# Who picks the place of a tile: the pool that hands out tiles, or the kernel's own plan

## Chip, core and metric

The kernel runs on one core of one Trainium2 chip. The metric is the device time of one execution in microseconds (us); the time before is the median of three runs.

## What is computed

All arrays are float32. Attention with a sigmoid instead of a softmax runs over 4 batches of 12 heads, 448 tokens and 64 columns a head. Its output, seen as 1792 tokens by 768, goes through two feed-forward layers.

```python
scores = scale * np.matmul(q, k.transpose(0, 1, 3, 2)) - np.log(S)
attn = 1.0 / (1.0 + np.exp(-scores))
x = np.matmul(attn, v)                                # then (B*S, 768)
...
xn = x / np.sqrt(np.mean(x * x, -1, keepdims=True) + 1e-06) * rms_g
g = xn @ w_gate                                       # 768 x 1536
y = ((g / (1.0 + np.exp(-g))) * (xn @ w_val)) @ w_out # 1536 x 768
...
h = y @ w_in                                          # 768 x 2048
out = (h - np.tanh(h)) @ w_out2                       # 2048 x 768
```

## The kernel before

**The work.** Attention (some 150 us) takes the heads in pairs; the rest of the time goes to five kinds of job: `Ag` and `Av` (gate and value), `B` (the first layer's output), `C` and `D` (the second layer). Each kind runs for batches 0 and 1 and then for batches 2 and 3. A matrix product of 2 by 2 blocks is mostly made with seven block products instead of eight, from sums and differences of the blocks (`S1` to `S4` of the weights, `T1` to `T4` of the tokens). Each float32 operand is split into a high and a low part, and a product takes three matmuls of 128 x 128 by 448 columns (lines 1081, 1136, 1161). TensorE (PE) does these; ScalarE (ACT) and VectorE (DVE) split operands, form sums, empty the PSUM banks and apply the functions.

**The transfers.** SyncE (SP) issues loads and most stores in the order of its queue: raw weights (line 488), prepared weights that were put into DRAM and come back (stores at lines 589 and 632, loads at 636, 644 and 672), spilled tokens (line 875). GpSimd (POOL) issues the loads and stores of the weights of the second products (`wB`, `wD`, line 589) and the sums that a DMA adds up in DRAM (`sumB`, `sumD`, `out`, line 959).

**The places.** A tile stands in one place of four pools: `unit` has 72 places of 128 x 448, `part` 20 of 128 x 768, `raw` 2, and `ps` the 8 PSUM banks. In the program's names, part_3881 is one `part` tile. When a new tile takes the place of an old one, its first writer waits until the last instruction that used the old tile is done; for an old tile that a DMA stores, until that DMA has landed.

**The order.** `Plan` keeps each piece of work with what it reads and writes. `lay` replays the work with a modelled duration for each piece and a table of ranks (`ORDER`), and gives each piece an engine and a start; the pieces are then issued in the order of these starts. For the places it counts: per pool a sorted list of the times, in its model, at which places come free. It takes the earliest, but which place of the chip a tile stands in it doesn't say. Line 409 asks a pool of 72 places under one tag for a tile, and the layer that hands out tiles picks one:

```python
return Slot(kind, lambda: pool.tile(shape, dt, tag=tag, name=tag))
```

Of the kernel before, what the change touches and what calls it, by code (L numbers as in the profile page):

```python
# [9 lines left out]
F32 = mybir.dt.float32  # L10
# [7 lines left out]
PSUM = bass.MemoryType.PSUM  # L18
# [4 lines left out]
P = 128  # L23
# [22 lines left out]
N_UNIT, N_MOE, N_RAW, N_PART = 72, 40, 2, 20  # L46
# [15 lines left out]
def numbers(text):  # L62
    d = [DIGITS[c] for c in text if c in DIGITS]
    return [4096 * d[i] + 64 * d[i + 1] + d[i + 2] for i in range(0, len(d), 3)]


class Slot:


    def __init__(self, kind, make):  # L70
        self.kind, self.make, self.tile = kind, make, None
        self.uses = []

    def __getitem__(self, part):
# [3 lines left out]
class Plan:  # L78
# [21 lines left out]
    def issue(self):  # L100
        work = self.work
        self.graph()
        for n, e in self.lay([ORDER_UNIT * n for n in numbers(ORDER)]):
            for s in self.slots[n]:
                s.tile = s.tile or s.make()
            work[n][1](e)

    def graph(self):
# [19 lines left out]
    def lay(self, rank):  # L128

        work, needs, users, slots, n_work = self.work, self.needs, self.users, self.slots, len(self.work)  # L130
        missing = [len(ds) for ds in needs]
        end, where, start_of = [None] * n_work, [None] * n_work, [None] * n_work
        taken, since = set(), {}
        kind_order = {}
        for n in range(n_work):
            for s in slots[n]:
                if s.kind and s.uses[0] == n:
                    kind_order.setdefault(s.kind, []).append(s)
        kind_at = {k: 0 for k in kind_order}
        free = {pool: [0.0] * size for pool, (size, _) in self.room.items()}  # L140
        held = {k: 0 for k in kind_order}
        pool_of = {k: pool for pool, (_, kinds) in self.room.items() for k in kinds}
        cap = {k: c for _, kinds in self.room.values() for k, c in kinds.items()}
        streams = {}
        for n, w in enumerate(work):
            if w[4]:
                streams.setdefault(w[4], []).append(n)
        stream_at = {s: 0 for s in streams}
        left = {}
        clock = {e: 0.0 for e in self.ENGINES}  # L150
        port = moving = 0.0
        waiting = sorted(n for n in range(n_work) if not missing[n])
        oldest, done = 0, [False] * n_work
        issued = 0

        def places(n):

            t, want = 0.0, {}
            for s in slots[n]:
                if not s.kind:  # L160
                    continue
                if s in taken:
                    t = max(t, since[s])
                    continue
                k = s.kind
                i = kind_at[k] + want.get(k, 0)
                if kind_order[k][i] is not s:
                    return None
                want[k] = want.get(k, 0) + 1
            for k, x in want.items():  # L170
                if held[k] + x > cap[k]:
                    return None
                f = free[pool_of[k]]
                if len(f) < x:
                    return None
                t = max(t, f[x - 1])
            return t

        while issued < n_work:
            cands = []  # L180
            while done[oldest]:
                oldest += 1
            for n in waiting:
                if n > oldest + self.WINDOW:
                    break
                engines, _, _, _, stream, _ = work[n]
                if stream and streams[stream][stream_at[stream]] != n:
                    continue
                if n > oldest + self.CLOSE and any(s.kind in self.CLOSELY and s not in taken for s in slots[n]):
                    continue  # L190
                t_place = places(n)
                if t_place is None:
                    continue
                ways = []
                for e, (ns, uses_port) in engines.items():
                    r = t_place
                    for d in needs[n]:
                        r = max(r, end[d] + (self.OTHER if where[d] != e else self.SAME if e != "PE" else 0))
                    if uses_port:
                        r = max(r, port)  # L200
                    start = max(clock[e], r)
                    ways.append((start + ns, start, n, e, uses_port))
                cands.append(min(ways, key=lambda w: w[0]))
            if not cands:
                raise RuntimeError(f"no work can start; the oldest is {oldest}")
            soonest = min(c[1] for c in cands) + SOON
            finish, start, n, e, uses_port = min((c for c in cands if c[1] <= soonest), key=lambda c: rank[c[2]])
            clock[e] = finish
            if uses_port:
                port = finish  # L210
            if work[n][5]:
                moving = max(finish + self.BEGIN, moving) + work[n][5]
                end[n] = moving + self.LAND
            else:
                end[n] = finish
            start_of[n], where[n], done[n] = start, e, True
            waiting.remove(n)
            for s in slots[n]:
                if s in taken:
                    continue  # L220
                taken.add(s)
                if s.kind:
                    kind_at[s.kind] += 1
                    held[s.kind] += 1
                    since[s] = free[pool_of[s.kind]].pop(0)
            for s in slots[n]:
                left[s] = left.get(s, len(s.uses)) - 1
                if s.kind and not left[s]:
                    held[s.kind] -= 1
                    bisect.insort(free[pool_of[s.kind]], max(end[u] for u in s.uses) + self.OTHER)  # L230
            if work[n][4]:
                stream_at[work[n][4]] += 1
            for u in users[n]:
                missing[u] -= 1
                if not missing[u]:
                    bisect.insort(waiting, u)
            issued += 1
        return [(n, where[n]) for n in sorted(range(n_work), key=lambda n: (start_of[n], n))]
# [127 lines left out]
def tile_sigmoid_attention_moe_moe(  # L366
# [16 lines left out]
    ENG = {"PE": nc.tensor, "ACT": nc.scalar, "DVE": nc.vector, "POOL": nc.gpsimd, "SP": nc.sync}  # L383

    const = ctx.enter_context(tc.tile_pool(name="const", bufs=1))
    unit_p = ctx.enter_context(tc.tile_pool(name="unit", bufs=N_UNIT))
    raw_p = ctx.enter_context(tc.tile_pool(name="raw", bufs=N_RAW))
    part_p = ctx.enter_context(tc.tile_pool(name="part", bufs=N_PART))
    norm_p = ctx.enter_context(tc.tile_pool(name="norm", bufs=4))
    ps_p = ctx.enter_context(tc.tile_pool(name="ps", bufs=8, space=PSUM))  # L390
    dram_p = ctx.enter_context(tc.tile_pool(name="spill", bufs=1, space=DRAM))

    plan = Plan({
# [12 lines left out]
        return {e: ({"SP": 400, "ACT": 540, "POOL": 870 if added else 540}[e], False)}  # L406

    def slot(kind, pool, shape, dt, tag):
        return Slot(kind, lambda: pool.tile(shape, dt, tag=tag, name=tag))

    def bank(kind="mm"):
        return slot(kind, ps_p, [P, 512], F32, "ps")

    def unit(kind, dt=F32):
        return slot(kind, unit_p, [P, S], dt, "unit")

    def part_of(kind, shape, dt=F32):
        return slot(kind, part_p, shape, dt, "part")
# [26 lines left out]
    def whole_bank(ps):  # L445

        nc.tensor.matmul(ps[:, :S], lhsT=mark[:, :P], rhs=mark, start=True, stop=True)
# [12 lines left out]
    for names, ph in (  # L460
# [3 lines left out]
        for bs in BATCHES:  # L464
            n = n_sets(ph)
# [768 lines left out]
    nc.gpsimd.memset(ones, 1.0)  # L1234

    for n in range(N_WARM):
        warm = ps_p.tile([P, 512], F32, tag="ps", name="ps")
        whole_bank(warm)
    nc.scalar.activation(expo[:, 0:1], ones[:, 0:1], AF.Sigmoid)
    nc.gpsimd.memset(expo, -0.5)  # L1240
# [74 lines left out]
    for j in range(len(jobs)):  # L1315
        ahead = conv(j + AHEAD) + rows_late.get(j - ROWS_AT, []) + [lambda: load(j + 2 * AHEAD)]
        plan.copies_by = "ACT"
        kind = kind_of(j)
# [5 lines left out]
        n = 2 if kind == PLAIN else HELD  # L1324
# [73 lines left out]
```

## Time and profile before

| | us |
|---|---|
| median of three runs (lowest to highest) | 1031.68 (1030.65 to 1034.58) |
| the profiled execution, its own time | 1031.29 |
| its span, from the first to the last instruction | 1029.5 |
| PE busy with matmuls | 1015.3 |
| DVE busy | 789.7 |
| ACT busy | 675.0 |
| POOL busy | 153.6 |

1.8 us of the profiled execution's time lie outside its span. The mean granted clock of PE was 0.996 of full speed. Engines work at the same time, so the busy times don't add up; idle time of an engine counts where the busiest one, PE, waits for it.

### The profile page before, as it was taken

The page shows a single profiled execution, that of the slowest core. Times are in us where ns is not written, and L with a number is a line of the kernel's source. Part 1 is how long each engine was busy: PE and PEld are TensorE (multiplying, and loading weights), DVE is VectorE, ACT ScalarE, POOL GpSimd, SP SyncE. Part 2 cuts the span into 40 slices and gives each one's busy share as a digit, 9 for nine tenths or more (in the row PEclk, how much of TensorE's full clock was granted, in tenths as well). Part 3 has the DMA queues.
Part 4 walks back from the last instruction along what each step waited for, and adds up shares of the span by engine and source line. Part 5 has one row for each costly group of instructions (what it writes and reads, how often), then busy time and mean ns, then how long its engine had stood idle before and what let it go on. Part 6 is the DMA issues. An engine that isn't in the chain of part 4 may idle for free.

```text
span 1029.5 us, 15331 instructions
## 1 busy us (share of the span) xinstructions
PE 1015.3 (99%) x5261; PEld 878.5 (85%) x5261; DVE 789.7 (77%) x1284; ACT 675.0 (66%) x1232; POOL 153.6 (15%) x217
## 2 busy tenths in 40 slices
PE   9999999999998999999999999999999999999998
PEld 4555479999997999899999999999998999999997
DVE  5578998877865878886875857999787986675766
ACT  6777956676674566684774747877675766675742
POOL 4231010000040051111012030000303300003030
PEclk9999999999998999999999999999999999999999
DMA  9587578778689599879859479585949782749493
GB/s 325 199 319 266 195 250 290 255 235 315 217 223 331 199 219 344 301 253 404 313 187 245 138 138 306 179 317 166 256 129 285 214 245 61 253 114 209 124 225 135
DMA packets 102573, 241.41 MB, mean 234 GB/s; under 512 B 11520, under 2 KB 59712, under 8 KB 102496
## 3 DMA queue, kind: packets, MB, share of 16 engines
q1 hardware_dynamic: 77840, 172.53, 49.0%
q0 software_dynamic: 24512, 67.84, 26.2%
q8 instruction: 41, 0.67, 0.3%
q14 instruction: 36, 0.29, 0.1%
q10 hardware_dynamic: 144, 0.07, 0.0%
HBM read 150.74 MB, written 89.66 MB: 234 GB/s over the span
## 4 chain that ended last, share of the span: by engine, by line
PE 86%; issue 6%; DMA 4%; DVE 2%; POOL 1%; ACT 1%; SPq 0%; POOLq 0%; DVEq 0%
PE ps L1136 43%; PE ps L1081 28%; PE ps L814 6%; PE ps L757 5%; PE ps L1161 3%; DMA wD<-part 2%; DMA sumB<-unit 1%; PE ps L778 1%; PE ps L798 1%; POOL sumB L959 1%; DMA part<-in_qkt 1%; PE ps L850 0%; DVE unit L1017 0%; DVE part L522 0%; DVE unit L888 0%
## 5 line engine op out<-in xcount | busy, mean ns | idle before, releaser
L1136 PE MATMUL ps<-unit,part 128*128 128x448 f32 x2520 | 521.5, 365 | 7.6 <-ACT unit L439 5.0
L1136 PEld LDWEIGHTS ps<-unit,part 128*128 128x128 f32 x2520 | 473.2, 188 | 50.2 <-ACT unit L439 7.9
L1081 PE MATMUL ps<-unit,part 128*128 128x448 f32 x1512 | 311.4, 364 | 0.0
L1081 PEld LDWEIGHTS ps<-unit,part 128*128 128x128 f32 x1512 | 283.4, 187 | 22.3
L522 DVE TENSOR_TENSOR part<-part 128x768 fp32r<-128x768 f32 (+1 forms) x244 | 215.7, 890 | 64.9 <-ACT part L439 53.6
L439 ACT COPY unit<-ps 128x448 f32<-128x448 f32 x291 | 151.2, 540 | 127.7 <-PE ps L1136 57.3
L439 ACT CAST part<-part 128x768 fp32r<-128x768 f32 (+1 forms) x236 | 183.3, 788 | 30.9 <-DVE part L607 7.7
L888 DVE TENSOR_TENSOR unit<-unit 128x448 fp32r<-128x448 f32 x252 | 152.5, 619 | 34.5 <-ACT unit L439 18.1
L439 ACT CAST unit<-unit 128x448 fp32r<-128x448 f32 x257 | 143.3, 576 | 30.6 <-DVE unit L1000 11.9
L1017 DVE TENSOR_TENSOR unit<-ps,unit 128x448 f32<-128x448 f32 x168 | 104.0, 622 | 41.4 <-PE ps L1081 17.5
L766 ACT ACTIVATE unit<-ps 128x448 f32<-128x448 f32 x168 | 81.3, 582 | 25.9 <-PE ps L757 14.3
L893 DVE TENSOR_TENSOR unit<-unit 128x448 f32<-128x448 f32 x144 | 86.2, 619 | 5.8 <-DMA unit<-sumB 2.8
L511 DVE SCALAR_TENSOR_TENSOR part<-raw,zero 128x768 uint32<-128x768 uint32 x68 | 64.8, 953 | 31.4 <-ACT zero L439 18.7
L439 ACT CAST zero<-raw 128x768 f16<-128x768 bf16 x56 | 60.5, 1080 | 11.9 <-DMA raw<-in_w_out 4.2
L959 POOL DMA_DIRECT2D sumB<-unit x48 | 41.9, 958 | 156.7 <-ACT unit L439 101.8
L814 PE MATMUL ps<-unit,part 128*64 128x448 f32 x288 | 59.5, 547 | 0.5 <-ACT unit L766 0.5
L1161 PE MATMUL ps<-unit,part 128*128 128x448 f32 x288 | 59.2, 364 | 0.0
L1161 PEld LDWEIGHTS ps<-unit,part 128*128 128x128 f32 x288 | 54.0, 187 | 4.2
L959 POOL DMA_DIRECT2D out<-unit x36 | 30.9, 927 | 174.9 <-DVE unit L1017 165.7
L757 PEld LDWEIGHTS ps<-unit 64*128 64x128 f32 x396 | 35.7, 184 | 19.1 <-ACT unit L766 9.7
L757 PE MATMUL ps<-unit 64*128 64x448 f32 x396 | 47.9, 376 | 0.0
L439 ACT COPY ps<-ps 128x448 f32<-128x448 f32 x36 | 18.7, 520 | 43.4 <-PE ps L1136 43.3
(54 smaller groups left out, 491.8 us busy)
## 6 DMA issues: line engine op xcount, KB each, us to landing
raw<-in_w_out POOLq DMA_DIRECT2D x28, 768.0 KB, 7.4
part<-wD SPq DMA_DIRECT2D x56, 384.0 KB
part<-wB SPq DMA_DIRECT2D x36, 384.0 KB
part<-wC SPq DMA_DIRECT2D x33, 384.0 KB
raw<-in_w_in SPq DMA_DIRECT2D x16, 768.0 KB
wC<-part SPq DMA_DIRECT2D x30, 384.0 KB
sumB<-unit POOLq DMA_DIRECT2D x48, 224.0 KB, 8.8
wD<-part POOLq DMA_DIRECT2D x28, 384.0 KB, 6.4
```

The lines of the kernel that those rows point to most:

```text
L439: add(engines, lambda e: (nc.scalar.copy if e == "ACT" else nc.vector.tensor_copy)(to(), of()), reads, writes)
L522: add({**dve(n, psum=False), **pool(n)}, lambda e: ENG[e].tensor_sub(lo(), of(), hi().bitcast(F32)), [*reads, *kh], [*kl])
L757: nc.tensor.matmul(ps[i].tile[:, :S], lhsT=k_of(w, b, c, i), rhs=x.tile[rows, :S], start=q == 0, stop=q == len(terms) - 1)
L766: add(act(S, psum=True), lambda e: nc.scalar.activation(to.tile, ps.tile[:, :S], AF.Sigmoid, bias=-math.log(S), scale=1.0 / math.sqrt(D)), ...
L814: nc.tensor.matmul(ps.tile[HEADS[i], :S], lhsT=v_of(v, b, c, i), rhs=a[c][i].tile, start=opens and c == 0, stop=not opens and c == MAIN - ...
L888: add({**pool(S), **dve(S, psum=False)}, lambda e: ENG[e].tensor_sub(t["l"].tile, of.tile, t["h"].tile.bitcast(F32)), [of["t"], kh], [kl])
L893: add({**dve(S, psum=False), **pool(S)}, lambda e: ENG[e].tensor_sub(t.tile, x.tile, y.tile), [x["t"], y["t"]], [t["t"]])
L959: add(queue("POOL", True), lambda e: nc.gpsimd.dma_start(out=d.tile, in_=t.tile, accum_op=ALU.add), [t["t"], d["t"]], [d["t"]], moved=move ...
L1017: add(dve(S), lambda e: nc.vector.tensor_add(t.tile, ps.tile[:, :S], t.tile), [ps["t"], t["t"]], [t["t"]])
L1081: nc.tensor.matmul(ps.tile[:, :S], lhsT=part(a), rhs=x[b].tile, start=n in (1, 5) and kp == 0 and q == 0, stop=kp == n_kp - 1 and q == 2, ...
L1136: nc.tensor.matmul(ps.tile[:, :S], lhsT=part(a), rhs=x[b].tile, start=n in ((1, 2, 5) if opening else (1, 5)) and i == 0 and q == 0, stop= ...
L1161: nc.tensor.matmul(ps.tile[:, :S], lhsT=wt, rhs=a[p].tile, start=start and i == 0, stop=stop and i == 2, skip_group_check=True)
```

## The change

Every place gets a tag of its own with one buffer (`unit0` to `unit71`, and so on), and the plan's list of free places holds, beside the modelled time at which a place comes free, which place it is. A tile gets the place at the head of that list. The numbers of places in each pool, the table `ORDER` and the rules of the plan stay. New lines number two, so a line 439 of before is line 441 after.

```diff
-        self.kind, self.make, self.tile = kind, make, None
+        self.kind, self.make, self.tile, self.place = kind, make, None, None
...
-                s.tile = s.tile or s.make()
+                s.tile = s.tile or (s.make(s.place) if s.kind else s.make())
...
-        free = {pool: [0.0] * size for pool, (size, _) in self.room.items()}
+        free = {pool: [(0.0, -1, i) for i in range(size)] for pool, (size, _) in self.room.items()}
+        n_freed = 0
...
-                t = max(t, f[x - 1])
+                t = max(t, f[x - 1][0])
...
-                    since[s] = free[pool_of[s.kind]].pop(0)
+                    since[s], _, s.place = free[pool_of[s.kind]].pop(0)
...
-                    bisect.insort(free[pool_of[s.kind]], max(end[u] for u in s.uses) + self.OTHER)
+                    bisect.insort(free[pool_of[s.kind]], (max(end[u] for u in s.uses) + self.OTHER, n_freed, s.place))
+                    n_freed += 1
...
-    unit_p = ctx.enter_context(tc.tile_pool(name="unit", bufs=N_UNIT))
+    unit_p = ctx.enter_context(tc.tile_pool(name="unit", bufs=1))
...
-        return Slot(kind, lambda: pool.tile(shape, dt, tag=tag, name=tag))
+        return Slot(kind, lambda place: pool.tile(shape, dt, tag=f"{tag}{place}", name=tag))
...
-        warm = ps_p.tile([P, 512], F32, tag="ps", name="ps")
+        warm = ps_p.tile([P, 512], F32, tag=f"ps{n % 8}", name="ps")
```

In the built program every engine has the same instructions on the same tiles in the same order as before. What differs is the address of a tile and, with it, what its first writer waits for. Of the 1424 `unit` tiles and 804 `part` tiles, 431 and 309 follow the same older tile as before. Three places of the order show it. The names in brackets are what an instruction waits for: PE_49, Activation_49 and DVE_49 for work of that engine, DMAHW... for the landing of a DMA that SP issued, DMASW... for one that POOL issued.

ACT in the job that PE does at 330 us, before. part_3881 stands in the place of part_3736, which SP stores:

```order
L439 COPY ps_3870<-ps_3854 128x448 [waits PE_49]
L439 CAST unit_3876<-unit_3454 128x448 [waits DVE_49]
L439 CAST part_3881<-part_3821 128x768 [waits DMAHW4_49,Activation_49]
L439 CAST zero_80<-raw_3738 128x768 [waits DMAHW0_49,Activation_49]
L439 CAST part_3897<-part_3750 128x768 [waits DMAHW2_49]
L439 CAST unit_3904<-unit_3482 128x448 [waits DMASW2_49,DVE_49]
L439 CAST part_3914<-part_3756 128x768 [waits DMAHW3_49,DMAHW1_49]
L439 CAST unit_3923<-unit_3507 128x448 [waits DVE_49]
L439 COPY unit_3930<-ps_3885 128x448 [waits DMASW3_49,PE_49]
```

The same rows of the change:

```order
L441 COPY ps_3870<-ps_3854 128x448 [waits PE_49]
L441 CAST unit_3876<-unit_3454 128x448 [waits DVE_49]
L441 CAST part_3881<-part_3821 128x768
L441 CAST zero_80<-raw_3738 128x768 [waits DMAHW0_49,Activation_49]
L441 CAST part_3897<-part_3750 128x768 [waits DMAHW2_49]
L441 CAST unit_3904<-unit_3482 128x448 [waits DVE_49]
L441 CAST part_3914<-part_3756 128x768 [waits DMAHW1_49,DMAHW3_49,DMASW1_49,Activation_49]
L441 CAST unit_3923<-unit_3507 128x448 [waits DMASW2_49,DVE_49]
L441 COPY unit_3930<-ps_3885 128x448 [waits PE_49]
```

No instruction moved. The waits of part_3881 are gone (its place is now the one that part_3409 left, last read by a matmul); part_3914 has two waits more, and unit_3930 no longer waits for a DMA of POOL.

DVE in the job at 382 us, before. part_4460 stands in the place of part_4389, which POOL stores into `wD`:

```order
L888 TENSOR_TENSOR unit_4435<-unit_4193,unit_4428 128x448 [waits DMASW4_49,Activation_49]
L934 SCALAR_TENSOR_TENSOR unit_4197<-unit_4197,g_sb_75,unit_2967 128x448 [waits DMAHW6_49]
L511 SCALAR_TENSOR_TENSOR part_4460<-raw_4350,zero_80 128x768 [waits DMASW5_49,DMASW2_49,Activation_49]
L893 TENSOR_TENSOR unit_4465<-unit_4197,unit_4386 128x448 [waits DVE_49]
L893 TENSOR_TENSOR unit_4476<-unit_4197,unit_4127 128x448 [waits DMASW7_49]
```

The same rows of the change:

```order
L890 TENSOR_TENSOR unit_4435<-unit_4193,unit_4428 128x448 [waits Activation_49]
L936 SCALAR_TENSOR_TENSOR unit_4197<-unit_4197,g_sb_75,unit_2967 128x448 [waits DMAHW6_49]
L513 SCALAR_TENSOR_TENSOR part_4460<-raw_4350,zero_80 128x768 [waits DMASW2_49,Activation_49]
L895 TENSOR_TENSOR unit_4465<-unit_4197,unit_4386 128x448 [waits DMASW4_49,DVE_49]
L895 TENSOR_TENSOR unit_4476<-unit_4197,unit_4127 128x448
```

part_4460 no longer waits for DMASW5, the store of part_4389; DMASW2, the load of raw_4350, stays. Another DMA's wait moved from unit_4435 to unit_4465. The instruction at 430 us (part_4942, line 522) differs in the same way: its place is not that of part_4834, which POOL stores, any more.

SP in its queue around 350 us, before (spilled tokens, `x2` and `x3`, and prepared weights, `wAv` and `wAg`, come in):

```order
L644 DMA part_4191<-wAv_0_2047 128x768 [waits DMAHW4_49,PE_49]
L875 DMA unit_4193<-x2_5_1631 128x448 [waits DMAHW5_49]
L875 DMA unit_4197<-x3_5_2073 128x448 [waits DMAHW6_49]
L644 DMA part_4305<-wAv_0_2047 128x384 [waits DMAHW7_49,PE_49]
L644 DMA part_4458<-wAg_1_2179 128x768 [waits DMAHW0_49,DVE_49,Activation_49]
```

The same rows of the change:

```order
L646 DMA part_4191<-wAv_0_2047 128x768 [waits DMAHW4_49,PE_49]
L877 DMA unit_4193<-x2_5_1631 128x448 [waits DMAHW5_49,DMASW6_49,DVE_49]
L877 DMA unit_4197<-x3_5_2073 128x448 [waits DMAHW6_49,DMASW4_49,DVE_49]
L646 DMA part_4305<-wAv_0_2047 128x384 [waits DMAHW7_49,PE_49]
L646 DMA part_4458<-wAg_1_2179 128x768 [waits DMAHW0_49,PE_49]
```

Here waits were added. unit_4193 and unit_4197 now stand in places that DVE reads until later (that of unit_4197 is left by the instruction of line 945 at 353.77 us in the trace of before), and the two loads behind them queue behind that.

## Rows read from the trace of the kernel before

**Rows 1.** The page: the span, and busy time of each engine.

```profile
span 1029.5 us, 15331 instructions
PE 1015.3 (99%) x5261; PEld 878.5 (85%) x5261; DVE 789.7 (77%) x1284; ACT 675.0 (66%) x1232; POOL 153.6 (15%) x217
```

**Rows 2.** Stretches: us, busy (instructions) of each engine, PE's clock, DMA share, GB/s.

```profile
0.00:150.00 150.00, 147.33 (x991) 77.16 (x991) 113.09 (x219) 113.06 (x245) 30.96 (x56) 1.00 0.75 262
...
300.00:340.00 40.00, 35.44 (x165) 32.34 (x164) 23.70 (x38) 19.49 (x34) 7.17 (x10) 0.91 0.97 302
340.00:440.00 100.00, 98.08 (x484) 90.28 (x483) 81.98 (x128) 61.85 (x108) 23.98 (x37) 1.00 0.86 267
440.00:780.00 340.00, 339.99 (x1682) 314.86 (x1681) 263.37 (x410) 226.66 (x399) 46.16 (x61) 1.00 0.76 234
780.00:800.00 20.00, 18.93 (x92) 16.63 (x91) 15.91 (x29) 14.08 (x29) 4.33 (x5) 1.00 1.08 313
800.00:1029.50 229.50, 225.61 (x1115) 208.48 (x1113) 166.97 (x269) 138.33 (x257) 31.04 (x36) 1.00 0.64 174
```

**Rows 3.** Timeline of PE: start, us, work xcount [idle before <-who ended it].

```profile
317.79 8.05 PE L1136 MATMUL ps<-unit,part 128*128 128x448 f32 x39
330.40 5.88 PE L1136 MATMUL ps<-unit,part 128*128 128x448 f32 x17 [4.56 <-ACT unit L439]
...
385.29 4.92 PE L1136 MATMUL ps<-unit,part 128*128 128x448 f32 x23 [0.28 <-ACT unit L439]
...
433.30 0.87 PE L1136 MATMUL ps<-unit,part 128*128 128x448 f32 x3 [1.64 <-DVE unit L1017]
...
795.75 1.48 PE L1136 MATMUL ps<-unit,part 128*128 128x448 f32 x6 [0.91 <-DVE unit L1017]
```

**Rows 4.** Timeline of ACT, ahead of PE's stop at 330 us.

```profile
319.03 0.57 ACT L439 CAST unit<-unit 128x448 fp32r<-128x448 f32 x1
325.79 0.83 ACT L439 CAST part<-part 128x768 fp32r<-128x768 f32 x1 [6.19 <-DMA wAg<-part]
...
329.83 0.95 ACT L439 COPY unit<-ps 128x448 f32<-128x448 f32 x2
```

**Rows 5.** Timeline of SP, issues of DMAs, around 308 and 349 us.

```profile
308.12 0.98 SPq L644 DMA_DIRECT2D part<-wB  x2
309.15 1.47 SPq L589 DMA_DIRECT2D wAg<-part  x2
...
349.41 0.91 SPq L875 DMA_DIRECT2D unit<-x  x2
```

**Rows 6.** Timeline of DVE: instructions ahead of PE's stops at 385, 433 and 795.

```profile
382.18 0.96 DVE L511 SCALAR_TENSOR_TENSOR part<-raw,zero 128x768 uint32<-128x768 uint32 x1 [4.36 <-DMA wD<-part]
...
430.15 0.96 DVE L522 TENSOR_TENSOR part<-part 128x768 fp32r<-128x768 f32 x1 [3.28 <-DMA wD<-part]
...
785.45 1.16 DVE L888 TENSOR_TENSOR unit<-unit 128x448 fp32r<-128x448 f32 x2 [2.00 <-DMA out<-unit]
```

**Rows 7.** The chain of waits that ended last, three pieces: start, us, what.

```profile
299.19 11.73 DMA sumB<-unit
...
373.05 9.00 DMA wD<-part
...
419.65 10.31 DMA wD<-part
```

**Rows 8.** Waits of ACT and SP: us in total, times, longest us.

```profile
ACT part L439 <- DMA part<-wC: 1.5, 1, 1.5
ACT part L439 <- DMA part<-wD: 0.5, 1, 0.5
...
SPq L644 <- PE ps L1136: 114.3, 44, 8.4
```

**Rows 9.** Timeline of DVE, around the spilled tokens' loads.

```profile
353.77 0.62 DVE L945 TENSOR_TENSOR unit<-unit 128x448 fp32r<-128x448 f32 x1
...
374.08 0.68 DVE L934 SCALAR_TENSOR_TENSOR unit<-unit,g_sb 128x448 f32<-128x448 f32 x1
```

**Rows 10.** Line 439 on DVE: instruction xcount: ns least/median/most, first and last start.

```profile
L439 DVEq EVENT_SEMAPHORE  x8: 21/21/21, 13.6 to 996.0; - x8
```

More of the change, by code (lines that the diff above doesn't have):

```diff
@@ L385, in tile_sigmoid_attention_moe_moe @@
     const = ctx.enter_context(tc.tile_pool(name="const", bufs=1))
-    unit_p = ctx.enter_context(tc.tile_pool(name="unit", bufs=N_UNIT))
-    raw_p = ctx.enter_context(tc.tile_pool(name="raw", bufs=N_RAW))
-    part_p = ctx.enter_context(tc.tile_pool(name="part", bufs=N_PART))
+    unit_p = ctx.enter_context(tc.tile_pool(name="unit", bufs=1))
+    raw_p = ctx.enter_context(tc.tile_pool(name="raw", bufs=1))
+    part_p = ctx.enter_context(tc.tile_pool(name="part", bufs=1))
     norm_p = ctx.enter_context(tc.tile_pool(name="norm", bufs=4))
-    ps_p = ctx.enter_context(tc.tile_pool(name="ps", bufs=8, space=PSUM))
+    ps_p = ctx.enter_context(tc.tile_pool(name="ps", bufs=1, space=PSUM))
     dram_p = ctx.enter_context(tc.tile_pool(name="spill", bufs=1, space=DRAM))
```

## Prediction

> **What bounds the kernel now.** Read the page first: PE works 1015.3 of the span's 1029.5 us, and no other engine comes near [rows 1]. So only two things can shorten the time: PE's stops, and PE's speed while it works. The stretches say where they are [rows 2]. From 440 to 780 us PE stands still for 0.01 us in all; there the kernel is as fast as PE. Outside attention the stops are in three stretches: 300 to 340 (40.00 - 35.44 = 4.56 us), 340 to 440 (1.92) and 780 to 800 (1.07). The first has a second oddity: a clock of 0.91. The 2.67 us in the first 150 (attention and its start) and the 3.89 after 800 (with the tail behind the last matmul) I take as they are.
>
> Next, PE's timeline at these stops [rows 3]. Each ends with ACT or DVE, not with a DMA: PE waits for an operand or a bank that they are late with. So ask what made them late [rows 4, 6]. ACT stood still 6.19 us before a CAST of one `part` tile, until a DMA `wAg<-part` landed. DVE stood still 4.36 us and 3.28 us for `wD<-part`, and 2.00 us for `out<-unit`. Here is the point of the whole reading: these DMAs are stores. Their result is in DRAM, and ACT and DVE read nothing from DRAM. An instruction on them that waits for a store can only wait for the place of the tile that is being stored. The chain of waits agrees: in it stand pieces of 9.00 us and 10.31 us of `wD<-part` [rows 7], the flight of a store ahead of a stop of PE.
>
> **What the change does, step by step.** No instruction is added or moved, so every term is a wait that goes or comes.
>
> Stop at 330. SP issued the stores of line 589 from 309.15 [rows 5]; ACT waited for one until 325.79 [rows 4]. Behind its CAST, in ACT's queue, stood six instructions, the last a COPY at 329.83 that empties a PSUM bank; PE began at 330.40, when that was done. So ACT needs 329.83 - 325.79 = 4.04 us for the queue. PE had run dry at 317.79 + 8.05 = 325.84. In the build of the change the CAST has no wait at all. ACT was free at 319.03 + 0.57 = 319.60, so the queue can be through at 319.60 + 4.04 = 323.64, 2.2 us before PE is dry. What could hold it then are the two `part<-wB` loads whose tiles are read in this queue, issued at 308.12 [rows 5]. When they landed no row says. Bounds: if only at 325.79, the gain is nothing; if with the flight of a DMA issued just before, 11.73 us [rows 7], at 319.9 to 320.4, which costs ACT under 1 us of the 2.2. I take the second, because that flight is of the same stretch: the full **4.56 us**.
>
> Its echo. After the stop 17 matmuls took 5.88 us, where 39 before it took 8.05, or 0.206 each [rows 3]. At that pace 17 take 3.51. The difference of **2.37 us** is the lower of the clock's two levels, 1.2 GHz instead of 2.4, granted for a few us after PE had stood still; the 0.91 of the stretch is its trace [rows 2]. The stops of 1.64 and 0.91 us left no such mark (clock 1.00). With the long stop this goes too.
>
> Stops at 385 and 433. DVE's instructions there wait for `wD` stores of POOL, and in the build of the change part_4460 and part_4942 no longer do. part_4460 still waits for the load of its raw weights; when that landed no row says, only that the store came last. If it came just before, nothing is gained, else the whole stop, and of DVE's 4.36 us the last 0.28 are enough: **0.28**. For part_4942, 3.28 us of DVE's delay against **1.64** of PE's stop [rows 3, 6]: half of it is enough.
>
> Stop at 795. The stores are sums added up in `out`; DVE's wait of 2.00 us is more than PE's stop of **0.91**. The tiles concerned get places that a matmul or DVE itself has left.
>
> Sum: 4.56 + 2.37 + 0.28 + 1.64 + 0.91 = 9.76 us. From the profiled execution's 1031.29 us that is 1021.53; this execution is 0.4 us below the median, so the same sum from the median gives 1021.9. I take **1021.5 us**, as the 0.16 us left of 780 to 800 (1.07 - 0.91) point down.
>
> What the change adds. First, waits. SP's queue bears most: the loads of unit_4193 and unit_4197, issued at 349.41 [rows 5], will wait until DVE's instruction of line 945 at 353.77 is done, some 5 us later, and two `part` loads stand behind them. Their cover: the first reader, on DVE at 374.08 [rows 9], comes 24.7 us after the issue; with the 11.73 us of flight above (an estimate), 8 us of cover are left after the delay. So nothing, from this place. Loads of prepared weights are the same kind: SP waits 114.3 us, in 44 waits of at most 8.4, for places that matmuls still read, and yet ACT waited for the landing of such loads only twice, 2.0 us in all [rows 8]. Second, instructions that only carry a further wait: 21 ns each on DVE [rows 10], on engines with idle time; nothing.
>
> **A rule against it.** The stops could mean that there are too few places. The Trainium skill ("Perfetto Trace Analysis", Optimization Strategy) says that consistent bubbles on the engine that should be saturated can mean that SBUF or PSUM has no room for the next tile. By that rule a change that leaves the number of places alone would leave the time at 1031.3. The trace speaks against it: the bubbles are not consistent. PE stands still 0.01 us in 340 us with the same 72 and 20 places [rows 2].
>
> **The rivals.**
>
> *The stores go, the loads stay* (1028.5). In 300 to 340 the DMA engines are busy for 0.97 of the time [rows 2]. If the raw weights or `wB` tiles land no earlier than the store did, PE's long stop and its echo stay, and only 0.28 + 1.64 + 0.91 = 2.83 us go: 1028.5. For it: the share. Against: the flights above.
> The Trainium skill ("DMA: Bandwidth & Descriptors", Issuing engines are not separate DMA queues) says that all issuing engines share the same 16 DMA engines; by that rule an earlier load of SP slows a store of POOL, and the trace's one busy share for all queues fits.
>
> *The plan's choice is no better* (1031.3). The plan picks by its model's times; if its idea of when stores land is as far off as the layer's was, other tiles meet other stores. Against: in all three places shown, the new older tile was left by a matmul or by DVE.
>
> *SP's loads come too late* (slower). SP issues in order, so one late place holds all loads behind it. If a new place costs SP its longest wait of now, 8.4 us, beyond the cover, PE stops for up to 8.4 us and has the echo of 2.37: 1021.5 + 10.8 = 1032.3 for one such event, 1043 for two. It decides from the second on; one alone gives the gain back. For it: many new places are left by a later matmul. Against: the covers above.
>
> **How the numbers follow.** Stops go: 0.73, between 1019 (that rest, and half of the spread of the runs shown, 2 us) and 1024.5 (a third of the sum stays). Loads stay: 0.12. No better: 0.06. SP late: 0.09, of it 0.05 with two events or more. A change under 0.5%, 5.2 us, can hardly be told from none here. Faster needs 1026.5 or less: the first case and a little of the second, 0.75. Slower: 0.05. The rest, 0.20, is the same. The range leaves out the last two cases and a little below: 1018.5 to 1029.
>
> **What would show it.** Right: in the profile after, no idle time of PE over 1 us between 300 and 800 us, clock 1.00 from 300 to 340, and no ACT or DVE row that waits for `wAg`, `wD`, `wB`, `sumD` or `out` stores. Wrong: PE's stops still end with ACT or DVE, which now wait for loads (`part<-w...`, `raw`); or the page's chain holds SP's loads.

## Result and the profile after

The changed kernel takes 1021.03 us (median of five runs, 1020.75 to 1022.22); the kernel before took 1031.68 beside it (five runs, 1029.3 to 1034.58). The ratio is 0.99, with a 95% interval of 0.988 to 0.9921: faster, by more than the 0.5% that can be told from no change. One execution is left out of the figures of the experiments below: the kernel with the issue key took 1678.78 us once, at a granted clock of 0.56, and the only profile of that kernel is of this execution.

The page of the changed kernel, the rows that answer to [rows 1], and its shares of the chain by engine:

```profile
span 1018.7 us, 15352 instructions
...
PE 1012.3 (99%) x5261; PEld 877.6 (86%) x5261; DVE 790.8 (78%) x1284; ACT 675.8 (66%) x1232; POOL 153.4 (15%) x217
...
PE 97%; DMA 2%; ACT 0%; DVE 0%; issue 0%; ACTq 0%; SPq 0%
```

The span is 10.8 us shorter, and PE's busy time only 3.0 us (1015.3 - 1012.3). So some 7.8 us are stops that went, and the rest is work that PE does faster. The matmuls are as many as before; the 21 further instructions (15352 against 15331) are not among those counted as busy.

The stretches of the changed kernel, columns as in [rows 2]:

```profile
0.00:150.00 150.00, 148.26 (x995) 78.00 (x995) 113.84 (x219) 112.94 (x245) 30.95 (x56) 1.00 0.76 264
300.00:340.00 40.00, 39.33 (x195) 36.15 (x194) 28.58 (x45) 24.37 (x42) 6.93 (x9) 1.00 1.04 328
340.00:440.00 100.00, 99.98 (x495) 92.39 (x494) 85.09 (x131) 62.64 (x109) 25.58 (x40) 1.00 0.87 273
440.00:780.00 340.00, 339.94 (x1681) 314.86 (x1680) 263.09 (x411) 229.11 (x405) 48.83 (x63) 1.00 0.78 236
780.00:800.00 20.00, 20.00 (x100) 18.56 (x99) 17.56 (x30) 16.32 (x31) 1.27 (x2) 1.00 0.79 235
```

PE's idle time in 300 to 340 falls from 4.56 us to 0.67 and the clock there rises from 0.91 to 1.00; in 340 to 440 the idle time falls from 1.92 to 0.02, in 780 to 800 from 1.07 to nothing. From 440 to 780, where nothing was to be had, nothing came.

At the place of the long stop, the timeline of ACT in the changed kernel (start, us, work, idle before in brackets); it answers to [rows 4]:

```profile
318.20 0.57 ACT L441 CAST unit<-unit 128x448 fp32r<-128x448 f32 x1
318.67 0.84 ACT L441 CAST part<-part 128x768 fp32r<-128x768 f32 x1
319.41 1.07 ACT L441 CAST zero<-raw 128x768 f16<-128x768 bf16 x1
320.35 0.83 ACT L441 CAST part<-part 128x768 fp32r<-128x768 f32 x1
321.08 0.56 ACT L441 CAST unit<-unit 128x448 fp32r<-128x448 f32 x1
322.14 0.84 ACT L441 CAST part<-part 128x768 fp32r<-128x768 f32 x1 [0.50 <-DMA sumB<-unit]
322.88 0.56 ACT L441 CAST unit<-unit 128x448 fp32r<-128x448 f32 x1
323.35 0.96 ACT L441 COPY unit<-ps 128x448 f32<-128x448 f32 x2
```

The first CAST of a `part` tile starts at 318.67 with no wait, where it started at 325.79 after 6.19 us of waiting. The COPY that empties the bank starts at 323.35 instead of 329.83. And PE, in the changed kernel, runs on at the places that answer to [rows 3]:

```profile
311.71 18.77 PE L1138 MATMUL ps<-unit,part 128*128 128x448 f32 x92
331.15 11.19 PE L1138 MATMUL ps<-unit,part 128*128 128x448 f32 x54 [0.67 <-DVE unit L1019]
...
374.94 60.50 PE L1138 MATMUL ps<-unit,part 128*128 128x448 f32 x297
...
786.88 13.31 PE L1083 MATMUL ps<-unit,part 128*128 128x448 f32 x65
```

The first row covers the time of the long stop: 92 matmuls in one run at 0.204 us each. A stop of 0.67 us follows, and after it 54 matmuls take 11.19 us, 0.207 each: no slow pace. The third row covers the stops at 385 and 433 and has no bracket, nor has the fourth, where the stop at 795 was.

The stop of 0.67 us is new, and no store is behind it. In the changed kernel, the issue on SP, a piece of the chain of waits and DVE's timeline:

```profile
309.91 4.32 SPq L877 DMA_DIRECT2D unit<-x  x3
...
310.34 19.51 DMA unit<-x
...
329.88 0.69 DVE L936 SCALAR_TENSOR_TENSOR unit<-unit,g_sb 128x448 f32<-128x448 f32 x1 [1.09 <-DMA unit<-x]
330.48 0.62 DVE L1019 TENSOR_TENSOR unit<-ps,unit 128x448 f32<-128x448 f32 x1
```

The first of these DVE instructions in the kernel before:

```profile
335.63 0.68 DVE L934 SCALAR_TENSOR_TENSOR unit<-unit,g_sb 128x448 f32<-128x448 f32 x1
```

A load of spilled tokens was 19.51 us in flight. DVE waited 1.09 us for it, and behind that stood the instruction on line 1019 that PE waits for. The change didn't delay the issue: in the kernel before, SP began these three loads at 310.67. But there the reader came 5.75 us later, behind the long stop, and had no wait.

What is left are these waits of PE, ACT, DVE and SP (us in total, times, longest):

```profile
PE ps L1138 <- DVE unit L1019: 0.7, 1, 0.7
...
ACT unit L441 <- DMA sumD<-unit: 0.7, 1, 0.7
ACT part L441 <- DMA sumB<-unit: 0.5, 1, 0.5
DVE unit L1019 <- DMA out<-unit: 0.6, 1, 0.6
DVE part L609 <- DMA wAv<-part: 0.3, 1, 0.3
...
SPq L646 <- PE ps L1138: 108.8, 44, 7.1
SPq L646 <- PE ps L1083: 67.7, 18, 8.7
```

ACT and DVE still wait for a place that a store holds, but for 2.1 us in these four waits, none over 0.7. The same view of the kernel before has 44.9 us of such waits (ACT 21.5, DVE 23.4), the longest of them that of [rows 4].

**Where the 10.8 us came from.** Landmarks in the two chains of waits, by runs of matmuls that stand in both. In the kernel before:

```profile
150.63 51.16 PE ps L1136 x252
...
448.13 21.84 PE ps L1081 x108
...
797.84 21.84 PE ps L1081 x108
```

In the changed kernel:

```profile
150.10 51.16 PE ps L1138 x252
204.90 21.84 PE ps L1083 x108
...
439.08 21.84 PE ps L1083 x108
...
787.04 21.84 PE ps L1083 x108
```

The changed kernel is ahead by 0.53 us where the layers begin, by 9.05 at the second landmark (8.52 more: the three stops and the echo, less the new stop of 0.67), and by 10.80 at the third (1.75 more, the stop at 795). That is the whole difference of the spans, 1029.5 - 1018.7 = 10.8; from there to the end nothing changes. The 0.53 us are not the change's doing. The layers begin as early in the first experiment below, which shares places as the kernel before does,

```profile
150.12 51.16 PE ps L1180 x252
```

and as late as before, at 150.57, in the one that differs from the changed kernel by one tile long after attention. So 10.27 us of the 10.8 are left for the change.

### The profile page after: what moved, and what is told of

Same layout as the page of the kernel before. It is cut to its first block, busy times and chain, and to the rows that moved or that the text cites. A ratio compares the mean times of both kernels' runs of the same rounds, so it can differ in the third digit from the quotient of the medians.

```text
span 1018.7 us, 15352 instructions
## 1 busy us (share of the span) xinstructions
PE 1012.3 (99%) x5261; PEld 877.6 (86%) x5261; DVE 790.8 (78%) x1284; ACT 675.8 (66%) x1232; POOL 153.4 (15%) x217
## 4 chain that ended last, share of the span: by engine, by line
PE 97%; DMA 2%; ACT 0%; DVE 0%; issue 0%; ACTq 0%; SPq 0%
PE ps L1138 48%; PE ps L1083 30%; PE ps L1163 6%; PE ps L816 6%; PE ps L759 5%; DMA unit<-x 2%; PE ps L780 1%; PE ps L800 1%; PE ps L852 0%; PE ps L449 0%; ACT unit L441 0%; DVE unit L1019 0%; ACT unit L832 0%; DVE unit L936 0%; ACT unit L768 0%
## 5 line engine op out<-in xcount | busy, mean ns | idle before, releaser
L890 DVE TENSOR_TENSOR unit<-unit 128x448 fp32r<-128x448 f32 x252 | 153.0, 621 | 30.3 <-ACT unit L441 24.7
```

The costliest lines, as they stand in the source:

```text
L890: add({**pool(S), **dve(S, psum=False)}, lambda e: ENG[e].tensor_sub(t["l"].tile, of.tile, t["h"].tile.bitcast(F32)), [of["t"], kh], [kl])
```

## Experiments

Three theories were set against each other. **Waits:** the gain is that of the waits for stores at a few places, and follows the choice of the place. **Addresses:** the tiles' new addresses, or the tags, change the speed of the engines or of the DMAs. **Slack:** the plan's choice changes the waits everywhere a little, and the gain is a sum of many. Diffs are against the changed kernel unless said otherwise. All were timed beside the kernel before on the same chip; ratios are to it.

**The old sharing through the new tags.** A table gives each tile, in the order in which tiles are made, a place, so that each tile follows the same older tile as in the kernel before. Every wait is that of before; the tags are the new ones, and the addresses differ from before.

```diff
+    made = {tag: iter(places) for tag, places in PLACES.items()}
+
+    def next_place(tag):
+        return PLACE_OF.index(next(made[tag]))
...
-        return Slot(kind, lambda place: pool.tile(shape, dt, tag=f"{tag}{place}", name=tag))
+        return Slot(kind, lambda place: pool.tile(shape, dt, tag=f"{tag}{next_place(tag)}", name=tag))
```

> A table gives every tile the place that follows the same older tile as in the kernel before, but through the changed kernel's tags, so at other addresses. Every instruction waits for what it waited for before. If the gain is the waits for stores: no gain, 1031 to 1032 us, the stop of PE of 4 to 5 us near 330 and the half clock behind it. If the gain is in the addresses or in the tags themselves: 1021 to 1024.

Measured: 1031.69 us, ratio 1.0006 (0.9995 to 1.0017). The stretch with the long stop, in this kernel:

```profile
300.00:340.00 40.00, 34.79 (x160) 31.68 (x158) 22.53 (x35) 18.21 (x31) 7.14 (x9) 0.91 0.96 296
```

The stop is back (5.21 us idle), the clock of 0.91 with it, and the time is that of before. The tags and where the old sharing stands on the chip are worth nothing: the gain lies in who follows whom. The single stops are not the same to the tenth, though: with the same sharing the long one is 5.21 us here and 4.56 in the kernel before, and 340 to 440 has 1.04 us of idle time instead of 1.92. A term of less than 1 us can't be proved by one trace.

**The new places for one pool alone.** The same table, with the new sharing for `part` and the old for `unit` and `ps`; then the new for `unit` and the old for `part` and `ps`. A character is one tile's place. The diffs are against the kernel of the experiment above, each cut to the first line of the string that is exchanged.

```diff
     "part": (
-        "0JIHGFEDCBA9876543210IGFDBA8JFH6543EC210I97BJHF7D8GA53EC674D61I9J20H85GBFGC7A6D3E1J20I945BFGJH826AD3C790IE145BFGJDH83C2A"
+        "0123456789ABCDEFGHI045J297AC132FEGH680I4BD571329C5JAEH68F9GCIBD1F0435JE7289CIH6EABF04D1J72835GF0IH6E9C14AJBD728356GE9F0H"
```

> Places of the part tiles as in the changed kernel, all others as before. If the gain is the waits for stores: the stops at 330 (4.56 and 2.37 of clock), 385 (0.28) and 433 (1.64) go, the one at 795 (0.91) stays: 1022 to 1023.5 us. If it needs all pools, or comes from unit tiles or PSUM: 1027 or more.

Measured: 1022.88 us, ratio 0.9919 (0.9903 to 0.9936). Two stretches of this kernel:

```profile
300.00:340.00 40.00, 39.62 (x196) 36.40 (x196) 28.88 (x45) 24.66 (x42) 6.60 (x9) 1.00 1.05 332
...
780.00:800.00 20.00, 19.03 (x94) 17.12 (x93) 18.77 (x33) 17.23 (x35) 0.68 (x1) 1.00 0.67 218
```

The long stop is gone and the one at 795 stays (0.97 us idle): its store is `out<-unit`, a `unit` tile [rows 6]. The other way about:

```diff
     "unit": (
-        "0][></=*+_-zyxwvutsrq123456po789ABCDEFGHIJKLMnmlkjihgNOPQRSTUVWXfedcYZab0][></z_x*=+-ywu1t3vsrBpC6q2h45o7MlkE89ADFGHJ_gO"
+        "0123456789ABCDEFGHIJKLMNOPQRSTUVWXYZabcdefghijklmnopqrstuvwxyz-_+*=/<>[]01235479BD68ACHELGFXNYIJQRKMOPTSpailmUVWZbcdfoqs"
```

> Places of the unit tiles as in the changed kernel, all others as before. If the gain is the waits for stores: only the stop at 795 goes, 1029.5 to 1031 us, with PE's stop near 330 as it was. If a place of a unit tile was behind the stop at 330: 1022 to 1024.

Measured: 1029.14 us, ratio 0.9978 (0.9967 to 0.9988). The reverse shows in the same two stretches of this kernel:

```profile
300.00:340.00 40.00, 35.11 (x163) 32.05 (x162) 23.27 (x37) 18.89 (x32) 7.55 (x10) 0.91 0.97 299
...
780.00:800.00 20.00, 20.00 (x101) 18.54 (x100) 17.02 (x31) 14.63 (x29) 2.33 (x3) 1.00 1.04 293
```

In 340 to 440 PE is idle for 0.02 us with the new sharing for `part` and for 0.80 with the old one, so the stops there belong to `part`.

The 1029.14 us lie below the range that was expected, 1029.5 to 1031: the stop at 795 is worth more than its 0.91 us of idle time. Between the second and the third landmark this kernel gains the same 1.75 us as the change. Beside their common median of before, 1031.71, the two gains are 8.83 and 2.57 us. They add up to 11.4, against 10.65 for the change: two parts that hardly touch each other, as terms of a sum should be.

**One tile put back.** part_3881 takes part_3736's place again, and part_3919 the one that part_3881 had; from there on the two places G and J of the table are exchanged, so that only these two tiles have another predecessor than in the changed kernel.

```diff
-        "B0A32G1F7CJ8E465IHD930FA6IGEB829HDCF17A4J2538IHD04B6EG5FH9C12AD4783I061JGCEBA7495H382BDE0FG4J9I17A6CD2853GHB09FI61JA475D"
+        "B0A32J1F7CG8E465IHD930FA6IJEB829HDCF17A4G2538IHD04B6EJ5FH9C12AD4783I061GJCEBA7495H382BDE0FJ4G9I17A6CD2853JHB09FI61GA475D"
```

> The changed kernel with one exchange: part_3881 gets the place of part_3736 again, which SP stores, and part_3919 the place that part_3881 had. Two instructions have other waits. If one such wait is enough for the long stop: ACT waits about 6 us for a wAg store, PE stops for 4 to 5 us near 330, the clock falls after it, 1026 to 1028.5 us. If the long stop needed the other waits of its stretch too, or ACT had slack in the new order: 1021 to 1023.

Measured: 1027.6 us, ratio 0.9962 (0.9949 to 0.9974), 6.6 us above the changed kernel. ACT and PE in this kernel, by their timelines:

```profile
326.21 0.83 ACT L483 CAST part<-part 128x768 fp32r<-128x768 f32 x1 [6.97 <-DMA wAg<-part]
...
330.25 0.95 ACT L483 COPY unit<-ps 128x448 f32<-128x448 f32 x2
...
330.82 9.40 PE L1180 MATMUL ps<-unit,part 128*128 128x448 f32 x32 [5.34 <-ACT unit L483]
```

One tile's predecessor brings back the whole chain: the store, ACT's CAST, the COPY 4.04 us behind it, PE's stop and the slow clock after it (32 matmuls in 9.40 us, 0.294 each). It costs nearly what the prediction's first two terms say, 4.56 + 2.37 = 6.93, though the stop is longer here, 5.34, and the one of 0.67 us that the changed kernel has at 331 is not there. That is against the theory of slack: one wait of one tile, of the 2228 in the two pools, holds 6.6 of its 10.65 us.

**What the plan takes for the end of a store.** In the change the key of a free place is the modelled end of its last user, for a store the landing. Here a list of its own holds the places, with another key; the order of the work is as it was.

```diff
+    def over(self, n, start, end):
+        return start
...
+                    s.place = left_at[pool_of[s.kind]].pop(0)[2]
...
+                    bisect.insort(left_at[pool_of[s.kind]], (max(self.over(u, start_of[u], end[u]) for u in s.uses), n_freed, s.place))
```

> The plan picks the place whose older tile was left first, but by the time at which the last user starts, in the model: a store counts as done when it is issued. Order and modelled times as in the changed kernel. If it is the flight of stores that the change takes into account: the waits for stores come back on other tiles, 1029 us or more (the places may be worse than before's: up to 1045). If any fixed rule of the plan does as well as the changed kernel's: 1021 to 1023.

Measured: four of five executions from 1038.4 to 1041.08 us, ratio 1.0074 (1.005 to 1.0099): slower than before. By this key a place counts as free when its store starts, so it can be given away while the store is in flight. Where PE then stops no profile shows, so that this is the reason is argued only. The other direction, 8 us more for each store:

```diff
+    def over(self, n, start, end):
+        return end + (8000 if self.work[n][5] and self.work[n][2] else 0)
```

> As the changed kernel, but a place left by a store counts as free 8 us later than the model says, so stored tiles are reused later and the places of matmuls' tiles earlier. If the waits for stores are all gone already, nothing is left to gain: 1021 to 1022.5 us, and SP's waits for matmuls grow. If a rest of the stops was due to stores: 1019.5 to 1020.5. If SP's loads have little cover: 1024 or more.

Measured: 1021.69 us, ratio 0.9901 (0.9883 to 0.9919), as the change. More margin for stores buys nothing, so the plan's times are good enough here. In this kernel SP waits longer for places that matmuls hold, and PE doesn't feel it (its 1.1 us below are again the late load of spilled tokens, 19.76 us in flight here):

```profile
PE ps L1144 <- DVE unit L1025: 1.1, 1, 1.1
...
SPq L652 <- PE ps L1144: 166.4, 50, 8.2
```

**Other addresses, all waits as in the change.** The three pools are laid out in the opposite order. This was meant to close the question of addresses.

```diff
-    unit_p = ctx.enter_context(tc.tile_pool(name="unit", bufs=1))
-    raw_p = ctx.enter_context(tc.tile_pool(name="raw", bufs=1))
     part_p = ctx.enter_context(tc.tile_pool(name="part", bufs=1))
+    raw_p = ctx.enter_context(tc.tile_pool(name="raw", bufs=1))
+    unit_p = ctx.enter_context(tc.tile_pool(name="unit", bufs=1))
```

> The changed kernel with its three SBUF pools laid out in the opposite order: every SBUF tile at another address, every wait the same. If only waits count: 1021 us, as the changed kernel, within 0.2%. If the addresses count: another time, by 1 us or more.

Measured: 1012.58 us (1012.4 to 1012.97), ratio 0.9816 (0.9801 to 0.9831). The second of the two cases came true: with the same sharing of places, 8.5 us went. Where, the page (first fence) and the chain of waits (second) of this kernel show:

```profile
PE 1003.2 (99%) x5261; PEld 877.2 (87%) x5261; DVE 790.1 (78%) x1284; ACT 676.1 (67%) x1232; POOL 153.8 (15%) x217
```

```profile
204.35 21.60 PE ps L1083 x108
```

PE's busy time is 9.1 us shorter. No stop went (its idle time is 7.1 us, 6.4 in the changed kernel); each matmul takes less. 108 of them take 21.60 us, 200.0 ns each, where the kernel before and the changed one both take 21.84, or 202.2 ns. Over the 4320 matmuls of the layers (2520 on line 1138, 1512 on line 1083, 288 on line 1163) 2.2 ns are 9.5 us. So addresses do count, though not in the change itself, whose steps are those of before.

**Which property of the addresses.** First theory: how a `unit` tile's own start is aligned. 64 unused bytes a partition ahead of all pools shift everything.

```diff
+    pad = const.tile([P, 16], F32, name="pad")
+    nc.vector.memset(pad, 0.0)
```

> The changed kernel with 64 unused bytes in a partition ahead of its pools. The pools keep their order, every wait stays; unit tiles (the matmuls' moving operands) now start at whole multiples of 128 bytes, where they stood 64 bytes past one, and part tiles (the weights) 64 bytes past, where they stood on one. This is what the opposite order of the pools had by chance. If the step of a matmul hangs on where a tile starts: 1012 to 1013 us, 108 matmuls in 21.60 us. If it hung on the order of the pools or on how far apart they lie: 1021, and 21.84 us.

Measured: 1021.48 us, ratio 0.9908 (0.9894 to 0.9923); 108 matmuls in 21.84 us. The theory fell: a common shift does nothing. The same edit in the kernel before (the diff is against it):

```diff
+    pad = const.tile([P, 16], F32, name="pad")
+    nc.vector.memset(pad, 0.0)
```

> The kernel before, its tiles placed by the layer, with 64 unused bytes ahead of its pools. If the start of a tile and the waits for stores are two things that add up: the matmuls gain about 9 us and the stops stay, 1022 to 1025 us. If faster matmuls only wait longer for ACT and DVE: 1028 or more.

Measured: 1032.33 us, ratio 1.0002 (0.9992 to 1.0012); 21.84 again. Next, 64 unused bytes between the `raw` and the `part` pool (where the texts on record say behind the `unit` pool), which move `part` against `unit`, with the shift ahead of all pools:

```diff
+    gap_p = ctx.enter_context(tc.tile_pool(name="gap", bufs=1))
+    gap = gap_p.tile([P, 16], F32, name="gap")
+    nc.vector.memset(gap, 0.0)
...
+    pad = const.tile([P, 16], F32, name="pad")
+    nc.vector.memset(pad, 0.0)
```

> As the one above, with 64 more unused bytes between the unit and the raw pool's neighbours, so that unit and part tiles both start at multiples of 128 bytes. If the moving operand's start decides: 1012 to 1013 us. If part tiles 64 bytes past a multiple are what is fast: 1021.

Measured: 1028.74 us, ratio 0.9974 (0.9965 to 0.9983). And without it:

```diff
+    gap_p = ctx.enter_context(tc.tile_pool(name="gap", bufs=1))
+    gap = gap_p.tile([P, 16], F32, name="gap")
+    nc.vector.memset(gap, 0.0)
```

> 64 unused bytes behind the unit pool alone: unit tiles stand 64 bytes past a multiple of 128 as in the changed kernel, part tiles now too. If the moving operand's start decides: 1021 us as the changed kernel. If the weights' start decides: 1012 to 1013.

Measured: 1029.03 us, ratio 0.9975 (0.9966 to 0.9984). None of the cases expected came true for either. Both lose most of the gain, and by the speed of PE again. In the chain of the kernel with both pads:

```profile
205.98 22.04 PE ps L1088 x108
```

108 matmuls take 22.04 us, 204.0 ns each. What the two slow kernels have in common is the distance from a `unit` tile to a `part` tile, the two operands of a matmul. That forecasts the last one: 128 unused bytes between `raw` and `part` give the distance that the opposite order of pools had, to a multiple of 256.

```diff
+    gap_p = ctx.enter_context(tc.tile_pool(name="gap", bufs=1))
+    gap = gap_p.tile([P, 32], F32, name="gap")
+    nc.vector.memset(gap, 0.0)
```

> The changed kernel with 128 unused bytes behind the unit pool; the pools keep their order, every wait stays. The first part tile now lies 141504 bytes behind the first unit tile; modulo 256 that is 192, as where the pools lay in the opposite order, against 64 in the changed kernel and 128 in the two runs with 64 bytes between the pools. If the distance modulo 256 sets the step of a matmul: 1012 to 1013 us, 108 matmuls in 21.60 us. If the pools' order or a longer period set it: 1018 or more.

Measured: 1012.16 us (1011.71 to 1013.0), ratio 0.9811 (0.9791 to 0.9831). In the chain of this kernel:

```profile
204.68 21.60 PE ps L1086 x108
```

It is level with the opposite order of pools, ahead of both kernels, and keeps the order of the pools. Together, with the addresses read in the built programs (distance: start of the first `part` tile less that of the first `unit` tile, in bytes of a partition):

| kernel | distance | mod 256 | ns a matmul | us |
|---|---|---|---|---|
| the change | 141376 | 64 | 202.2 | 1021.03 |
| 64 ahead of all | 141376 | 64 | 202.2 | 1021.48 |
| 64 ahead of `part`, with or without 64 ahead of all | 141440 | 128 | 204.0 | 1028.74, 1029.03 |
| pools in opposite order | -73792 | 192 | 200.0 | 1012.58 |
| 128 ahead of `part` | 141504 | 192 | 200.0 | 1012.16 |

A `unit` tile is 1792 bytes long and a `part` tile 3072, both multiples of 256, and the 128-column slices of a `part` tile are 512 bytes apart; so every matmul with a `unit` and a `part` operand has the same distance to a multiple of 256 in one layout. Neither operand's start alone sorts the table: with 64 and with 128 bytes ahead of `part`, `unit` tiles start where they do in the changed kernel, and with 64 ahead of all, `part` tiles start where they do with 64 ahead of `part` alone.

## Why the prediction was right, point by point

**The reading.** ACT and DVE waited for places that stores held, and PE for ACT and DVE. Putting one tile back shows it for the long stop, in every link. The two pools apart show which stops belong to `part` and which to `unit`.

**The stop at 330 and its echo.** Forecast 4.56 + 2.37. The queue was through at 323.35, forecast 323.64; that the two are so near is luck, as ACT was free for it 0.8 us earlier than in the kernel before and took 4.7 us instead of 4.0. At 325.84, where PE had run dry, it now runs on. The bound "nothing is gained, if the `part<-wB` loads land late" is excluded: the first CAST that reads one of them, at 320.35, doesn't wait, and the second, at 322.14, waits 0.50 us for a store. 0.67 us of idle time are new, the late load of above. The echo went in full, clock 1.00, and came back with the one tile.

**The stops at 385 and 433.** Forecast 0.28 + 1.64; both went, and 340 to 440 has 0.02 us idle. The load of raw weights that part_4460 still waits for was there: in the changed kernel DVE's instruction has no idle time before it.

```profile
370.91 0.95 DVE L513 SCALAR_TENSOR_TENSOR part<-raw,zero 128x768 uint32<-128x768 uint32 x1
```

For the second landmark the terms, less the new stop, give 4.56 + 2.37 + 0.28 + 1.64 - 0.67 = 8.18 us; 8.52 were measured.

**The stop at 795.** The mechanism was right, the size was not: forecast 0.91, measured 1.75. The rest of the 1.07 us of idle time went too, and a stop costs PE more than the idle time says: from 783.29 to 797.84 of before it took 14.55 us for what takes it 12.74 in the changed kernel (774.30 to 787.04), and of these 1.81 us only 1.07 are idle. (0.06 were given back between the landmarks.) Some 0.3 of the other 0.74 us, by an estimate, are a matter of counting: the last matmul ahead of a stop counts as busy for its whole 0.36 us, though the next would have followed after 0.20, and there are two stops here. Most of the rest are slower matmuls. In the kernel before:

```profile
788.92 4.10 PE L1136 MATMUL ps<-unit,part 128*128 128x448 f32 x18 [0.17 <-ACT unit L439]
```

At the usual step these 18 take 3.80 us. Why they are slower, at a clock of 1.00, isn't shown.

**The sum.** As measured it is 8.52 + 1.75 = 10.27 us, against 9.76. It was 0.84 us short at the stop at 795 and 0.33 too long up to the second landmark, where the new stop was missing from it. The 0.53 us of the start are the difference of two executions. The median of 1021.03 lies 0.5 below the forecast.

**What the change adds.** Forecast: nothing. The waits that it gives SP cost nothing that shows. The loads of unit_4193 and unit_4197 show it best. In the changed kernel SP issues them here, and DVE first uses one here (timelines of SP and DVE):

```profile
349.46 0.85 SPq L877 DMA_DIRECT2D unit<-x  x2
...
367.19 0.68 DVE L936 SCALAR_TENSOR_TENSOR unit<-unit,g_sb 128x448 f32<-128x448 f32 x1
```

By the clock of the program the issue stayed, while the reader came 6.9 us earlier [rows 9]. The cover shrank from 24.7 us to 17.7, and that was enough, but not for the reason given: the prediction took 11.73 us for the flight of such a load, and the one that came late at 330 was 19.51 us in flight, more than these 17.7. SP's longest wait behind a matmul is 8.7 us, and PE shows no stop from it.

What the forecast of nothing left out is that a load can come late without being delayed, because its reader comes earlier once a stop is gone. That cost 0.67 us at 331. Where the long stop is back, with the old sharing or the one tile, DVE's instruction, at 335.92 and 336.43, has no wait. The rival of late loads came about in this small form, not by the places that it named.

**The other rivals.** That the loads would land no earlier than the stores did: the DMA share in 300 to 340 is now 1.04, more than the 0.97 of before, at 328 GB/s instead of 302, and no load ended a wait of ACT in the rows above; the one that DVE waited for cost the 0.67 us. The Trainium skill ("DMA: Bandwidth & Descriptors", Issuing engines are not separate DMA queues) says that DMAs started by different engines run on the same 16 DMA engines. The profile gives one share for all of them, which fits, but no run here tests it. That the plan's choice is no better: excluded by the result; the issue key shows a choice by the plan that is worse.
The Trainium skill ("Perfetto Trace Analysis", Optimization Strategy) says that consistent bubbles can mean too few places. The stops here were of another kind: with the same 72 and 20 places, idle time in 300 to 440 fell from 6.48 to 0.69 us.

**What was forecast wrongly in what to look for.** "No ACT or DVE row that waits for stores" was too strong: four such waits of 0.3 to 0.7 us remain, and no stop of PE in the rows above comes from them. And one sign of being wrong did show, in small: a stop of PE that ends with DVE, which waits for a load.

## What to carry to other kernels

An instruction that waits for a store though it reads nothing from DRAM waits for a place. Before buying more places, see which older tile stood there: a place left by a matmul or by the engine itself, instead of one that is being stored, was worth 1% here, and one single tile 6.6 us. Such a choice needs an estimate of when the store lands; counting it as done when it starts was worse than leaving the choice to the pool. And when a stop goes, everything behind it comes earlier: a load that was hidden behind the stop can be the next to be late, here for 0.67 us.

## What the hardware showed that was not expected

The step of back-to-back matmuls (128 x 128 weights, 448 columns, float32 rounded to the matmul's format) depended on the distance in SBUF between its two operands: 202.2, 204.0 and 200.0 ns for distances of 64, 128 and 192 bytes to a multiple of 256, at a granted clock of 1.00 in all. Over this kernel that is 1021, 1029 and 1012 us, a spread as large as one and a half times the change under study, with the same matmuls in the same order and the same sharing of places (the unused bytes add a memset or two). A common shift of all tiles did nothing. That the distance sorts all the layouts tried is shown; why is not, and a distance of 0 was not tried. Whoever compares two kernels whose pools differ in size or order should first look at the step of a run of matmuls in both: if it differs, part of the difference is the layout's.
